# Reordering the first loads, the key transposes and one weight load in a fused adaLN attention and SwiGLU block

## The chip, the cores and the metric

The kernel runs on one core of one Trainium2 chip. The metric is device time in microseconds (us) of one execution, lower is better. Each run lists its mean granted TensorE clock.

The engines are called PE (TensorE), DVE (VectorE), ACT (ScalarE), POOL (GpSimd) and SP (the queue that issues most of the DMAs).

## The reference

All tensors are bfloat16. There are 2048 tokens of width 1024, 32 query heads and 4 key/value heads of width 128, a window of 512 keys, and a feed-forward width of 3584. Cut to what matters:

```python
mod = (silu(c) @ w_mod).reshape(1, 6, 1, -1)          # sa, ca, ga, sb, cb, gb
h = layernorm(x) * (1 + ca) + sa
q = h @ wq                                            # 32 heads of 128
k, v = k_cache[..., -512:, :], v_cache[..., -512:, :] # 4 heads, each used by 8 query heads
x = x + ga * (softmax(q @ k.T * 128**-0.5) @ v @ wo)
h = layernorm(x) * (1 + cb) + sb
x = x + gb * ((silu(h @ w_gate) * (h @ w_up)) @ w_down)
```

## The kernel before

The tokens are worked in four chunks of 512. The query weights `wq` come in groups of four heads (1 MB each). Keys must be transposed ("turned") once on PE, four 128x128 blocks for each of the 4 key groups, by way of one PSUM bank, `XB`. An iteration `i` of the attention loop computes scores of head `i-1` and the weighted values of head `i-2`, and projects a later head.

For the first chunk the projections of heads 0 to 7 start before the shift `sa` is known; their bias `wq.T @ sa` is added later, from the "bias columns" (matmuls of one column each). The parts that matter, with cuts:

```python
def wq_slot(gidx):                       # which of three SBUF slots a query group goes to
    return NWQ if gidx == 2 else gidx % NWQ          # NWQ = 2
...
for hf in range(2):                      # the loads at the start, all from SP, in order
    load_wca(hf); load_wq0(hf)
load_wq(1)
load_k(0)
for k2 in range(DT // 2):
    load_wsa(k2)
load_v(0)
load_wq(2)                               # 1 MB, third query group (heads 8 to 11)
load_x(1)                                # 1 MB, second tokens
for gk in range(1, Hkv):
    load_k(gk)                           # 128 KB each
for gk in range(1, Hkv):
    load_v(gk)
...
qproj_mm(7, QB0[7], 0, HK)               # just before the loop
q_bias_mm(0, 2, BB); q_shifted(0)        # bias columns of heads 0, 1, copied by DVE
qproj_mm(7, QB0[7], HK, DT); q_raw(7); q_shifted(1)
for dt in range(DT):
    shift(dt)                            # eight DVE operations, add sa to the input
...
for i in range(1, NA + 2):
    if i % 4 == 1 and i > 5 or i == 6:
        load_wq((i + 3) // 4 + 1)        # i == 6 loads the fourth query group (heads 12 to 15)
    ...
    for gk in {2: (1,), 3: (2, 3)}.get(i, ()):
        k_turn(gk, XB)                   # PE, into bank XB
        T.op(DVE, lambda: V.tensor_copy(kd, ks), writes=[PB[XB], B_kT[gk]])
    ...
    if i == 1: scores(0)
    if i in (1, 3, 5):
        q_bias_mm(i + 1, i + 3, QB)      # bias columns of the next two heads, in bank QB
    if i > NQ0: qproj(i + LEAD)          # NQ0 = 8, LEAD = 3
    elif i % 2 == 0: qproj(NQ0 - 1 + i // 2)   # i == 2 projects head 8, into bank QB
    ...
    scores(i - 1); pv(i - 2); run_bg(1)
```

The softmax here doesn't subtract the row's maximum and nothing guards it: scores larger than these inputs give would overflow.

## Time and profile before

| what | value |
|---|---|
| time, median of the first 3 runs | 1278.99 us (1278.6 to 1279.32) |
| span of the profiled execution | 1277.5 us |
| PE busy | 1259.3 us, 99% of the span |
| mean granted PE clock in that execution | 1.000 |

The first part of the page gives the busy time of each engine, its share of the span and its instructions.

```profile
PE 1259.3 (99%) x7541; PEld 646.0 (51%) x7683; DVE 480.1 (38%) x897; ACT 341.8 (27%) x388; POOL 42.2 (3%) x102
```

PE is the bound, so only the time that PE stands idle can be won by reordering. The list of waits of PE says for what it stood idle: total us, times, longest.

```profile
PE ps L272 <- DMA arena<-in_A_k_cache_dram: 2.2, 1, 2.2
PE ps L268 <- POOL arena L407: 2.2, 1, 2.2
PE ps L268 <- DMA arena<-in_A_wq_dram: 1.6, 2, 0.9
PE ps L272 <- DVE arena L853: 1.6, 1, 1.6
```

Line 268 is the helper of all matmuls, line 272 that of the PE transposes. The timeline of PE shows where these waits are (start, length, engine, line, operation, count, and in brackets the idle time before it and its releaser).

```profile
30.29 0.54 PE L268 MATMUL ps<-mod_bf,arena 128*128 128x1 bf16 x16
33.07 0.40 PE L272 MATMUL ps<-arena 128*128 128x128 bf16 x4 [2.24 <-DMA arena<-in_A_k_cache_dram]
33.30 3.66 PE L268 MATMUL ps<-arena 128*128 128x512 bf16 x27
36.80 0.39 PE L272 MATMUL ps<-arena 128*128 128x128 bf16 x4
38.78 0.38 PE L272 MATMUL ps<-arena 128*128 128x128 bf16 x4 [1.59 <-DVE arena L853]
...
44.67 0.54 PE L268 MATMUL ps<-mod_bf,arena 128*128 128x1 bf16 x16
...
57.52 1.90 PE L268 MATMUL ps<-arena 128*128 128x512 bf16 x7 [0.71 <-DMA arena<-in_A_wq_dram]
59.25 0.34 PE L268 MATMUL ps<-sc_bf,arena 128*128 128x1 bf16 x8
```

There are three stalls after 30 us (the POOL wait and the 0.9 us wait for a query load lie before 14 us, and the change does not touch them). At 30.8 us the turn of key group 1 (iteration 2) waits for its load. At 37.2 us the second of two turns in one bank (iteration 3) waits for DVE to copy out the first. At 56.8 us the projection of head 12 waits for the fourth query group. The timeline of DVE shows why the second took long: the copy of the turned keys (L853) stands in a queue.

```profile
37.00 0.18 DVE L774 RECIPROCAL rl<-ps 128x4 f32<-128x4 f32 x1 [1.08 <-PE ps L268]
37.22 0.69 DVE L777 TENSOR_TENSOR arena<-ps,rl 128x512 bf16<-128x512 f32 x1
37.83 0.47 DVE L665 TENSOR_SCALAR arena<-arena,bq 128x512 bf16<-128x512 f32 x1
38.22 0.41 DVE L853 COPY arena<-ps 128x512 bf16<-128x512 bf16 x1
```

The timeline of the SP queue shows when the two loads were issued.

```profile
22.99 3.03 SPq L384 DMA_DIRECT2D arena<-in_A_k_cache_dram  x3
...
49.51 0.52 SPq L354 DMA_DIRECT2D arena<-in_A_wq_dram  x1
```

Key group 1 landed 10.0 us after issue and the fourth query group 8.0 us after.

### The profile page before, as it was taken

How to read it: one execution, taken by the hardware profiler on the slowest of the kernel's cores; microseconds unless marked ns; L12 is line 12 of the kernel's file. 1: busy time of each engine (PE TensorE's matmuls, PEld its weight loads, DVE VectorE, ACT ScalarE, POOL GpSimd, SP SyncE). 2: the span in 40 equal slices, each digit the busy share in tenths (PEclk: the TensorE clock that was granted, in tenths of full speed). 3: DMA queues.
4: the chain of work that ended last, by engine and by line, in shares of the span. 5: the costliest groups of instructions: out<-in, count | busy, mean ns of one | idle time of the engine just before them, and what ended most of it. 6: DMA issues, size and time to landing. Idle time of an engine off the chain costs nothing.

```text
span 1277.5 us, 17800 instructions
## 1 busy us (share of the span) xinstructions
PE 1259.3 (99%) x7541; PEld 646.0 (51%) x7683; DVE 480.1 (38%) x897; ACT 341.8 (27%) x388; POOL 42.2 (3%) x102
## 2 busy tenths in 40 slices
PE   8899999999999999999999999999999999999999
PEld 5565545555455564465554444444444444444444
DVE  4555325765247652265422322233222331222222
ACT  4555303555025550055510111011100111011100
POOL 1011000000000010000000000000000000000000
PEclk9999999999999999999999999999999999999999
DMA  9899403977018741054252974046421654035200
GB/s 323 225 234 247 104 1 79 194 142 165 1 22 183 155 104 42 4 129 113 71 148 83 277 233 131 25 145 160 136 71 47 196 145 132 17 116 165 66 9 25
DMA packets 235854, 155.31 MB, mean 122 GB/s; under 512 B 129024, under 2 KB 222080, under 8 KB 235776
## 3 DMA queue, kind: packets, MB, share of 16 engines
q1 hardware_dynamic: 177520, 95.45, 31.4%
q10 hardware_dynamic: 58256, 58.73, 14.6%
q8 instruction: 60, 0.98, 0.3%
q14 instruction: 18, 0.15, 0.0%
HBM read 119.54 MB, written 4.19 MB: 97 GB/s over the span
## 4 chain that ended last, share of the span: by engine, by line
PE 96%; SPq 2%; DMA 1%; issue 1%; DVE 0%; ACT 0%
PE ps L268 96%; DMA arena<-in_A_k_cache_dram 1%; DMA arena<-in_A_wq_dram 1%; SPq L331 0%; SPq L299 0%; SPq L354 0%; SPq L384 0%; SPq L363 0%; SPq L306 0%; SPq L358 0%; ACT arena L756 0%; DVE rl L774 0%; PE ps L272 0%; SPq L389 0%; DVE arena L777 0%
## 5 line engine op out<-in xcount | busy, mean ns | idle before, releaser
L268 PE MATMUL ps<-arena 128*128 128x512 bf16 (+2 forms) x7236 | 1251.8, 333 | 11.5 <-POOL arena L407 2.2
L268 PEld LDWEIGHTS ps<-arena 128*128 128x128 bf16 x7378 | 635.8, 98 | 620.5 <-issue 2.5
L756 ACT ACTIVATE arena<-ps 128x1024 bf16<-128x1024 f32 x256 | 262.2, 1024 | 353.8 <-PE ps L268 342.1
L988 ACT ACTIVATE arena<-ps 128x512 bf16<-128x512 f32 x112 | 66.9, 597 | 506.4 <-PE ps L268 506.4
L989 DVE TENSOR_TENSOR arena<-ps,arena 128x512 bf16<-128x512 f32 x112 | 77.5, 692 | 276.6 <-PE ps L268 276.6
L796 DVE TENSOR_TENSOR tmp<-ps,rowb 128x512 f32<-128x512 f32 (+1 forms) x65 | 44.4, 683 | 318.7 <-PE ps L268 318.7
L639 DVE CAST arena<-ps 128x512 bf16<-128x512 f32 x120 | 83.0, 692 | 54.8 <-PE ps L268 54.8
L777 DVE TENSOR_TENSOR arena<-ps,rl 128x512 bf16<-128x512 f32 x128 | 88.5, 691 | 4.7 <-DVE rl L774 0.3
L774 DVE RECIPROCAL rl<-ps 128x4 f32<-128x4 f32 x128 | 23.4, 183 | 119.0 <-PE ps L268 119.0
L414 DVE BATCH_NORM_STATS2 st<-x_res 128x6 f32<-128x512 bf16 x62 | 42.3, 683 | 3.5 <-DMA x_res<-in_A_x_dram 3.4
L419 POOL TENSOR_SCALAR rstd<-mv 128x1 f32<-128x1 f32 x28 | 6.3, 227 | 891.7 <-DVE mv L418 891.7
L584 DVE SCALAR_TENSOR_TENSOR arena<-arena 128x1024 bf16<-128x1024 bf16 x24 | 29.2, 1215 | 0.0
L798 DVE TENSOR_TENSOR arena<-tmp,x_res 128x512 bf16<-128x512 f32 (+1 forms) x33 | 22.3, 676 | 1.1
L798 DVE TENSOR_TENSOR x_res<-tmp,x_res 128x512 bf16<-128x512 f32 x32 | 22.1, 692 | 1.1
L430 DVE TENSOR_SCALAR arena<-arena,gain,mod_bf 128x512 bf16<-128x512 bf16 x56 | 20.3, 405 | 0.0
L425 DVE TENSOR_SCALAR nsc<-x_res,mv,rstd 128x1024 bf16<-128x1024 bf16 x30 | 16.0, 534 | 0.0
L421 POOL TENSOR_TENSOR rstd<-rstd,mhalf 128x1 f32<-128x1 f32 x28 | 15.8, 565 | 2.3
L599 POOL TENSOR_SCALAR arena<-arena,c 128x128 bf16<-128x128 bf16 x24 | 14.4, 618 | 32.7 <-PE ps L268 32.4
L268 PEld LDWEIGHTS ps<-sc_bf,arena 128*128 128x128 bf16 x192 | 6.7, 96 | 2.3
L268 PE MATMUL ps<-sc_bf,arena 128*128 128x1 bf16 x192 | 6.8, 163 | 0.1
L272 PE MATMUL ps<-arena 128*128 128x128 bf16 x32 | 3.1, 218 | 3.8 <-DMA arena<-in_A_k_cache_dram 2.2
L418 DVE BATCH_NORM_AGGREGATE mv<-st 128x2 f32<-128x12 f32 x28 | 5.8, 209 | 1.0
(53 smaller groups left out, 50.4 us busy)
## 6 DMA issues: line engine op xcount, KB each, us to landing
arena<-in_A_wq_dram SPq DMA_DIRECT2D x31, 1024.0 KB, 6.1
arena<-in_B_w_gate_dram ACTq DMA_DIRECT2D x28, 1024.0 KB, 5.4
arena<-in_B_w_up_dram ACTq DMA_DIRECT2D x28, 1024.0 KB, 8.2
arena<-in_A_wo_dram SPq DMA_DIRECT2D x8, 1024.0 KB, 7.1
arena<-in_B_w_down_dram SPq DMA_DIRECT2D x7, 1024.0 KB, 8.7
out_dram<-arena SPq DMA_DIRECT2D x15, 256.0 KB, 2.0
x_res<-in_A_x_dram SPq DMA_DIRECT2D x3, 1024.0 KB, 7.7
arena<-in_w_mod_dram SPq DMA_DIRECT2D x8, 256.0 KB, 6.3
```

The lines of the kernel that those rows point to most:

```text
L268: T.op(PE, lambda: TE.matmul(out_ap, lhsT, rhs, start=start, stop=stop, skip_group_check=skip), reads=reads, writes=[bank_buf])
L414: T.op(DVE, lambda: V.bn_stats(st_[sl][:, hf * 6:hf * 6 + 6], x_res[:, t, hf * 512:hf * 512 + 512]), reads=[B_x[t]], writes=[B_st[sl]])
L430: T.op(DVE, lambda: V.tensor_scalar(dst[:, dt, :], dst[:, dt, :], gain[gi][:, dt:dt + 1], mod_bf[:, ccol + dt:ccol + dt + 1], op0=ALU.mult ...
L584: T.op(DVE, lambda: V.scalar_tensor_tensor(mt[n % 2], mt[n % 2], 1.0, sc_row, op0=ALU.mult, op1=ALU.mult, accum_out=mcol[:, n:n + 1]), rea ...
L639: T.op(DVE, lambda: V.tensor_copy(qT_s[qs], bank(b)), writes=[PB[b], B_qT[qs]])
L756: T.op(ACT, lambda: A.activation(ex_s[es][:, 2 * kp:2 * kp + 2, :], banks2(SCB + 2 * kp), AF.Exp, scale=att_scale), writes=[PB[SCB + 2 * k ...
L774: T.op(DVE, lambda: V.reciprocal(rl[r][:, :].rearrange("p (a b) -> p a b", a=2), psap(PVB * 512 + P, [[512, 2], [130, 2]])), writes=both + ...
L777: T.op(DVE, lambda: V.tensor_tensor(o_s[os_].rearrange("p (a b) d -> p a b d", a=2), psap(PVB * 512, [[512, 2], [130, 2], [1, P]]), rlb, A ...
L796: T.op(DVE, lambda: V.tensor_tensor(tmp[s][:, 0:n], bank(b, n), rowb[ri][:, c0:c0 + n], ALU.mult), reads=[B_row[ri]], writes=[PB[b], B_tmp ...
L798: T.op(DVE, lambda: V.tensor_tensor(dst[:, c0:c0 + n], tmp[s][:, 0:n], x_res[:, t, c0:c0 + n], ALU.add), reads=[B_tmp[s], B_x[t]], writes= ...
L988: T.op(ACT, lambda: A.activation(sg_s[ss], bank(gb), AF.Silu), writes=[PB[gb], B_sg[ss]])
L989: T.op(DVE, lambda: V.tensor_tensor(guT[:, ft, :], bank(ub), sg_s[ss], ALU.mult), reads=[B_sg[ss]], writes=[PB[ub], B_gu[ft]])
```

## The change

Its intent is to take away the three stalls. Key group 1 is read before the third query group, and the second tokens last. One key group is turned per iteration, so that DVE has an iteration to empty the bank. The fourth query group goes into the first slot, whose last reader (the bias columns of heads 2 and 3) is in iteration 1, so it can be issued at iteration 4 instead of 6. Later groups alternate between the first two slots, as before but with the parity turned round.

```diff
             def wq_slot(gidx):
-                return NWQ if gidx == 2 else gidx % NWQ
+                return gidx if gidx <= NWQ else (gidx + 1) % NWQ
@@
             load_v(0)
+            load_k(1)
             load_wq(2)
-            load_x(1)
-            for gk in range(1, Hkv):
+            for gk in range(2, Hkv):
                 load_k(gk)
             for gk in range(1, Hkv):
                 load_v(gk)
+            load_x(1)
@@
-                if i % 4 == 1 and i > 5 or i == 6:
-                    load_wq((i + 3) // 4 + 1)
+                if i % 4 == 1 and i > 5 or i == 4:
+                    load_wq((i + 4) // 4 + 1)
@@
-                for gk in {2: (1,), 3: (2, 3)}.get(i, ()):
+                for gk in {2: (1,), 3: (2,), 4: (3,)}.get(i, ()):
```

## The prediction

> **What bounds it now.** TensorE: the busy table gives 1259.3 us of a 1277.5 us span (99%), granted clock full, and PE is 96% of the chain of waits. Only idle PE time near the start can be won: the table by stretches shows 3.96 us idle between 30 and 40 us, 0.84 us between 50 and 60 us. The list of waits and the PE timeline name three stalls:
> 1. 30.83 to 33.07 us: the turns (PE transposes) of key group 1, iteration 2, wait for its DMA (2.24 us). Issued at 22.99 us behind wq group 2 and the second tokens (1 MB each), it took 10.0 us.
> 2. 37.2 to 38.8 us, iteration 3: groups 2 and 3 are turned in one bank; the second turn waits for the copy of the first, queued on DVE behind reciprocal 0.18, normalisation 0.69, shift 0.47, own copy 0.41 us. Idle 1.59 us.
> 3. 56.8 to 57.5 us: wq group 3, issued at 49.51 us, landed 8.0 us later; PE idle 0.71 us.
>
> **What changes.** Nothing is added or removed, only order. Key group 1 is issued before wq group 2; other keys and values before the second tokens; one turn moves from iteration 3 to 4; wq group 3 goes to slot 0, read last at iteration 1, and is issued at iteration 4.
>
> **DMA check.** [...] a 128 KB key load took 10.0 us behind megabytes. Key 1, now issued near 16.7 us, should land by 27 us, before 30.83. wq group 2 (landed 28.85) is pushed by 128 KB at 368 GB/s, 0.35 us: 29.2 us, before use near 31.9. Second tokens should land by about 34 us, read near 45. wq group 3: issued about 41, landed by 50, wanted about 53.
>
> **What each step is worth.**
> 1. Not all of 2.24 us. After the turn (0.23) comes head 8's projection into the bank of the bias matmuls, whose copy by DVE ends at 31.93 us behind eight shifts. So it starts at about 31.98 instead of 33.30 us: 1.3 us saved, and a new stall of about 0.7 us on DVE.
> 2. From turn to turn is 1.98 us; a free turn takes 0.22: 1.75 us saved. Exponentials (2.14 us a head on ACT) come close to limiting here; I allow 0.2 us lost.
> 3. 0.7 us saved.
> Sum about 3.6 us, all on the critical path, since PE has no large gaps afterwards and everything merely starts earlier.
>
> **Predicted time** 1275.4 us, 8 in 10 between 1273.8 and 1277.6 us. Faster by over 2%: 0.01; within 2%: 0.98; slower by over 2%: 0.01.
>
> **Signs.** Right: no PE wait on a key DMA; at iteration 2 a PE wait of 0.5 to 0.9 us on DVE (bias copy or shifts) after the turn; none on key copies at 35 to 40 us; none on wq at 50 to 60 us; PE idle from 30 to 60 us down from about 5 to about 1.3 us; PE busy still near 1259 us. Wrong: PE waits on wq group 2 at 31 to 33 us, on ACT at 36 to 40 us, or DVE statistics waiting for second tokens near 45 us.
>
> **What would make it wrong.** wq group 2 later than its margin of 2.7 us; stall 2 returning as a wait on score banks held by ACT (0.5 us at 45.7 us now); the gate columns (1 MB) and wq group 3 colliding near 40 us and delaying head transposes and the modulation matmuls of iteration 7. Any of these would shrink the gain to 2 us or less; none costs a per cent.

One clause of the DMA check is cut from the record. No term of the sum (1.3, 1.75 less 0.2, and 0.7 us, about 3.6 us) rested on it, and the landing of key group 1 near 27 us is an estimate from its issue near 16.7 us and the 10.0 us of the first trace.

## The result, and the profile after

The changed kernel took 1275.52 us (median of 4 runs, 1275.35 to 1275.87); the kernel before took 1279.15 us (median of 4, 1278.6 to 1280.52). The ratio is 0.997, 95% interval 0.9953 to 0.9988: within 2%, and faster. Ratios here are the mean time of one kernel's runs over that of the other's in the same rounds, so they are not quite the ratio of the medians quoted.

The span fell from 1277.5 to 1273.8 us. The busy line of the page after:

```profile
PE 1267.0 (99%) x7683; PEld 645.7 (51%) x7683; DVE 479.6 (38%) x897; ACT 341.5 (27%) x388; POOL 42.0 (3%) x102
```

PE busy time rose by 7.7 us although no matmul was added. The count behind it explains that: the trace before has 7541 PE records and the trace after 7683, as many as there are weight loads in both. 142 matmul records are missing from the first trace, and PE busy time may not be compared between these two.

The waits of PE after:

```profile
PE ps L268 <- POOL arena L408: 2.2, 1, 2.2
PE ps L268 <- DVE bq L661: 1.0, 1, 1.0
PE ps L268 <- DMA arena<-in_A_wq_dram: 0.7, 1, 0.7
```

The wait on the key load and the wait on the copy between turns are gone. The 0.7 us on a query load that is left is an older one between 9 and 14 us, which was 0.9 us in the trace before. A new wait of 1.0 us on DVE has come up. The timeline of PE after, at the same places:

```profile
30.39 0.54 PE L268 MATMUL ps<-mod_bf,arena 128*128 128x1 bf16 x16
30.80 0.38 PE L272 MATMUL ps<-arena 128*128 128x128 bf16 x4
32.17 3.66 PE L268 MATMUL ps<-arena 128*128 128x512 bf16 x28 [0.99 <-DVE bq L661]
35.66 0.39 PE L272 MATMUL ps<-arena 128*128 128x128 bf16 x4
...
38.07 0.39 PE L272 MATMUL ps<-arena 128*128 128x128 bf16 x4
...
41.79 0.54 PE L268 MATMUL ps<-mod_bf,arena 128*128 128x1 bf16 x16
...
55.49 0.34 PE L268 MATMUL ps<-sc_bf,arena 128*128 128x1 bf16 x8
```

And the issue of key group 1, on SP, which now lands 10.1 us later, at 26.8 us:

```profile
16.69 2.88 SPq L384 DMA_DIRECT2D arena<-in_A_k_cache_dram  x1
```

To keep the three steps apart I use four marks that all these kernels share in the timeline of PE: A, the bias columns of iteration 1 (30.29 us before); B, the projection of head 8 (33.30); C, the bias columns of iteration 5 (44.67); D, the first eight gate columns of iteration 9 (59.25). Step 1 lies between A and B, step 2 between B and C, step 3 between C and D.

| | A to B | B to C | C to D |
|---|---|---|---|
| before | 3.01 | 11.37 | 14.58 |
| after | 1.78 | 9.62 | 13.70 |
| gain | 1.23 | 1.75 | 0.88 |

The sum is 3.86 us; mark A was 0.10 us later in this execution, which leaves 3.76 us at mark D. The span is 3.7 us shorter. So everything after 60 us merely starts earlier: the two traces agree there, and the gain is neither lost nor increased later.

### The profile page after: what moved, and what is told of

Its sections match the earlier page's. It is cut to its first block, busy times and chain, and to the rows that moved or that the text cites. A ratio compares the mean times of both kernels' runs of the same rounds, so it can differ in the third digit from the quotient of the medians.

```text
span 1273.8 us, 17943 instructions
## 1 busy us (share of the span) xinstructions
PE 1267.0 (99%) x7683; PEld 645.7 (51%) x7683; DVE 479.6 (38%) x897; ACT 341.5 (27%) x388; POOL 42.0 (3%) x102
## 4 chain that ended last, share of the span: by engine, by line
PE 99%; DMA 1%; DVE 0%; SPq 0%; ACT 0%; issue 0%
PE ps L268 98%; DMA arena<-in_A_wq_dram 1%; DVE arena L671 0%; SPq L331 0%; SPq L306 0%; PE ps L272 0%; ACT arena L757 0%; DVE arena L666 0%; DVE tmp L797 0%; DVE arena L799 0%; DVE bq L661 0%
## 5 line engine op out<-in xcount | busy, mean ns | idle before, releaser
L268 PE MATMUL ps<-arena 128*128 128x512 bf16 (+1 forms) x7378 | 1260.7, 334 | 4.0 <-POOL arena L408 2.2
L640 DVE CAST arena<-ps 128x512 bf16<-128x512 f32 x120 | 82.9, 691 | 53.8 <-PE ps L268 53.8
L653 DVE COPY arena<-ps 128x512 f32<-128x512 f32 x4 | 2.7, 688 | 8.3 <-PE ps L268 8.3
```

The lines of the kernel that those rows point to most:

```text
L268: T.op(PE, lambda: TE.matmul(out_ap, lhsT, rhs, start=start, stop=stop, skip_group_check=skip), reads=reads, writes=[bank_buf])
L640: T.op(DVE, lambda: V.tensor_copy(qT_s[qs], bank(b)), writes=[PB[b], B_qT[qs]])
```

## The experiments

The theory is that there are three separate stalls, each removed by one part of the change. The rivals are that the parts only pay together, that ACT or the DMA takes the gain back, or that something later in the kernel is the cause. A fourth question came up: why the times of the kernel before spread much more than those of the changed one.

### Each part alone

The load order alone (the second hunk of the diff, on the kernel before):

> Only the order of the first loads is that of the changed kernel (key group 1 before the third wq group, second tokens last). Theory of three separate stalls: the wait on the key DMA at 30.8 us is gone and a PE wait of about 1.0 us on the DVE bias copy stands in its place, so the projection of head 8 starts at 32.2 instead of 33.3 us, 1.1 us gained; the wait of 1.6 us for the copy of the second turn and the 0.7 us on the fourth wq group stay. Time 1.1 us below before. Rival (the parts only pay together, because PE catches up with the next late thing): a start earlier by 1.1 us is eaten by a longer wait at the double turn or on the fourth wq group (which lands at a fixed time), time within 0.4 us of before.

The turns alone (the last hunk):

> Only the turns are moved: one key group per iteration at 2, 3 and 4. Three separate stalls: the 2.24 us wait on the key DMA stays, the 1.6 us wait for the copy between two turns is gone, the bias matmuls of iteration 3 start 1.75 us earlier counting from the first turn; 1.75 us below before. Rival (exponentials on ACT limit these iterations): PE waits on ACT for score banks grow by about as much and the gain is under 0.7 us.

The fourth query group alone (the first and third hunks):

> Only the fourth wq group goes to the first slot and is loaded at iteration 4. Three separate stalls: the wait of 0.7 us at 57 us (0.9 on the weight load) is gone, nothing before it moves, 0.8 us below before. Rival (the load is DMA bound, its bytes collide with the gate columns and landings move out): the wait stays over 0.4 us, or a new wait on gate columns appears at 50 us, time within 0.3 us of before.

All three gave correct results. The kernel before, in the rounds of these runs, had a median of 1280.47 us (7 runs, 1278.57 to 1282.52).

| run | times, us | median | A to B | B to C | C to D |
|---|---|---|---|---|---|
| load order alone | 1277.9 to 1280.06 | 1278.32 | 1.78 | 11.36 | 14.95 |
| turns alone | 1276.89 to 1277.38 | 1277.11 | 1.96 | 9.63 | 15.03 |
| fourth group alone | 1277.33 to 1277.77 | 1277.69 | 2.37 | 11.36 | 13.70 |

Each part takes its own stretch to the value that the changed kernel has there (1.78, 9.62 and 13.70 us) and, but for two things told below, leaves the others alone. That the parts pay only together is refuted, and so is a gain taken back by ACT: the turns alone gave the full 1.74 us. The marks are used here, and not the times, because 5 of the 7 runs of the kernel before in these rounds had a lower clock (0.999 to 0.997, see below); against its two runs at full clock (1278.9 and 1278.57 us) the three medians are 0.4, 1.6 and 1.0 us lower.

Two numbers were not as expected. First, two of these kernels have the load order of before, yet they waited less for the key load than its first trace: A to B took 1.96 and 2.37 us instead of 3.01. Second, C to D grew where the fourth query group was not touched, from 14.58 to 14.95 and 15.03 us: when PE arrives earlier, part of the gain goes into a longer wait for that group. The rival of a longer wait for that group later on has a grain of truth, of about 0.4 us.

### How much of it is chance

The kernel before, unchanged, profiled again:

> The kernel before, unchanged, profiled once more. The first experiments that kept its load order waited 1.18 and 1.59 us for key group 1 where its own first trace shows 2.24 us. If the landing of that load varies from run to run, this trace shows a wait between 1.0 and 2.4 us at 30.8 us that is not 2.24, the other two stalls as before (1.6 us at the turn exactly, 0.6 to 1.2 us on the fourth wq group), and the times spread over more than 1 us. Rival (2.24 us is what the order costs, and the two parts each removed some of it): 2.2 us again and a spread under 0.7 us.

Its median was 1279.85 us (1278.64 to 1280.65, 4 runs); A to B took 2.35 us, with a wait of 1.57 us for the keys:

```profile
32.02 0.40 PE L272 MATMUL ps<-arena 128*128 128x128 bf16 x4 [1.57 <-DMA arena<-in_A_k_cache_dram]
```

B to C took 11.36 and C to D 14.90 us. So the wait for the key load varies from execution to execution with the landing of a load that sits behind megabytes: 2.24 us in the first trace, 1.57 here, 1.18 in the turns alone, 1.59 in the fourth group alone; it landed 10.0, 8.9, 9.3 and 8.9 us after its issue. The turn's stall is the same every time (B to C is 11.36 or 11.37 us in the four traces that have it). The first trace happened to show a large step 1 and a small step 3.

### Undoing one part

The changed kernel with the first loads in the old order:

> The changed kernel with the loads at the start in the old order (key group 1 after the second tokens). Separate stalls: a wait on the key DMA of 1.2 to 2.2 us at 30.8 us comes back in place of the 1.0 us on the bias copy, nothing else; 0.2 to 1.2 us slower than the changed kernel, and times that spread more. Rival (the order feeds later loads too): also a wait on the fourth wq group or on gate columns, over 1.5 us slower.

The changed kernel with the new slot but the old time of issue of the fourth query group:

```diff
-                if i % 4 == 1 and i > 5 or i == 4:
-                    load_wq((i + 4) // 4 + 1)
+                if i % 4 == 1 and i > 5 or i == 6:
+                    load_wq((i + 3) // 4 + 1)
```

> The changed kernel, with the fourth wq group still in the first slot but issued at iteration 6 as before. If what counts is when it is issued, the wait of PE on it comes back at 53 us, at 1.0 to 1.3 us (more than the 0.7 us of before, as PE arrives earlier after the two other stalls are gone), and the kernel is about 1.2 us slower than the changed one. Rival (what counts is the slot, whose old readers held the load back): wait under 0.3 us, time equal to the changed kernel.

The changed kernel with the second tokens back in their old place:

```diff
             load_k(1)
             load_wq(2)
+            load_x(1)
             for gk in range(2, Hkv):
@@
-            load_x(1)
```

> The changed kernel, with the second tokens loaded after the third wq group as before, so that only key group 1 goes ahead. With one turn per iteration, key group 2 is wanted at 35.7 us and should land at 33 to 34.5 us, so nothing waits and the time equals the changed kernel within 0.3 us: second tokens last is then worth nothing. Rival: a wait on the key DMA of up to 1 us at 35.7 us.

All were correct. The kernel before had a median of 1279.09 us in these rounds (7 runs).

| run | times, us | median | A to B | B to C | C to D |
|---|---|---|---|---|---|
| old load order | 1275.96 to 1277.57 | 1276.64 | 2.56 | 11.31 | 13.70 |
| fourth group issued late | 1276.27 to 1276.99 | 1276.79 | 1.78 | 9.62 | 15.21 |
| second tokens kept | 1275.06 to 1275.86 | 1275.31 | 1.78 | 9.62 | 13.70 |

The late issue brings this wait back, in the list of waits of PE of that run:

```profile
PE ps L268 <- DMA arena<-in_A_wq_dram: 1.3, 1, 1.3
```

It is what counts about the third part: with the new slot and the old time of issue C to D takes 15.21 us, so the early issue is worth 1.5 us by the traces, twice what the wait of 0.71 us before promised, and 1.1 us by the mean times (1276.71 against 1275.57, in different jobs). A wait in the list also tells a little less than it costs: in all five traces told of so far that have this wait, C to D exceeds 13.70 us by the listed wait plus 0.17 us (0.71 gives 0.88, 1.34 gives 1.51). The free first slot is only what allows that issue. Putting the second tokens last is worth nothing that these runs can see: with them in their old place the time is 1275.31 us against 1275.52.

With the old load order the wait for the key load came back in place of the one on DVE, and the mean time was 1.1 us longer than the changed kernel's (1276.70 against 1275.57), both as expected:

```profile
32.19 0.40 PE L272 MATMUL ps<-arena 128*128 128x128 bf16 x4 [1.79 <-DMA arena<-in_A_k_cache_dram]
```

But it gave a surprise. Its B to C took 11.31 us, 1.7 us more than the 9.62 us of the same turns, with no wait for an engine or a load to account for it. The stretches of that trace show it (stretch, length, then busy us and instruction counts of PE, weight loads, DVE, ACT and POOL, then the granted PE clock, the DMA share and GB/s):

```profile
25.00:30.00 5.00, 4.87 (x70) 2.79 (x70) 2.48 (x8) 0.97 (x2) 0.00 (x0) 1.00 1.07 368
30.00:35.00 5.00, 2.99 (x27) 1.50 (x25) 2.41 (x9) 1.68 (x2) 0.00 (x0) 0.75 0.98 281
35.00:40.00 5.00, 5.00 (x63) 3.39 (x62) 2.36 (x6) 3.09 (x4) 0.00 (x0) 0.91 0.14 52
```

The clock that PE was granted fell to 0.75 of full in the mean of the five microseconds that hold the end of the wait. In finer stretches it was 1.00 during the wait, 0.50 from 32.5 to 35.9 us, and then 1.00 again. The weight loads, one for each matmul, show the spacing:

```profile
32.19 0.23 PEld L272 LDWEIGHTS ps<-arena 128*128 128x128 bf16 x4 [1.87 <-DMA arena<-in_A_k_cache_dram]
...
33.20 0.15 PEld L268 LDWEIGHTS ps<-arena 128*128 128x128 bf16 x1 [0.28 <-issue]
33.63 0.15 PEld L268 LDWEIGHTS ps<-arena 128*128 128x128 bf16 x1 [0.28 <-issue]
...
35.76 1.83 PEld L268 LDWEIGHTS ps<-arena 128*128 128x128 bf16 x19 [0.28 <-issue]
```

They are 0.43 us apart until about 35.8 us, where matmuls of this size otherwise are about 0.22 us apart (the eight of head 12's projection take 1.90 us, the last drawn 0.38 us long). So at a granted clock of 0.50 the spacing doubled, for 3.4 us. The drop followed a wait of 1.79 us here, while in the first trace of the kernel before a wait of 2.24 us was not followed by one (granted clock 1.00 in every stretch from 28 to 41 us). Whether the wait brought it about, this trace alone does not tell.

### Is the spread of the kernel before the clock?

Since each run lists its mean granted clock, all 29 later runs of the kernel before can be sorted by it (25 beside other kernels, 4 of its second profiling).

| mean granted clock | runs | times, us | mean, us |
|---|---|---|---|
| 1.000 | 15 | 1278.33 to 1279.8 | 1278.88 |
| 0.999 to 0.997 | 14 | 1280.06 to 1283.48 | 1280.88 |

The two heaps do not overlap: about half of the executions have a lower clock, and they take 2.0 us longer. Twelve of them, at 0.999 and 0.998, average 1280.53 us, 1.65 us above the others, which is about what the one slow stretch in the trace above cost (1.7 us); the two at 0.997 took 1282.52 and 1283.48 us. None of these slower executions was profiled, so whether one of the three stalls lets the clock drop, and which, is not shown. All 4 runs of the changed kernel have 1.000, but so have the 8 runs of "turns alone" and "fourth group alone", which keep the wait for the key, while one of the 4 runs of "load order alone", which does not have it, was at 0.998 (1280.06 us). Four runs each are too few to tell. Whether a wait can bring the drop about is tested by filling the wait with work.

The kernel before, with matmuls on zeros ahead of the turn at iteration 2 (a second line keeps the zeros safe from a later load into their place):

```diff
+                if i == 2:
+                    warm(6, XB)
                 for gk in {2: (1,), 3: (2, 3)}.get(i, ()):
@@
-                    for b_ in B_qT[NQT:]:
+                    for b_ in B_qT[NQT:] + [B_zw]:
```

> The kernel before, with 6 matmuls on zeros (about 1.3 us) put in front of the turn of key group 1 at iteration 2, where PE otherwise idles for its DMA. The times of the kernel before fall in two heaps, near 1278.7 and near 1280.6 us, and the profile of the changed kernel with late keys shows PE at half rate (matmuls 0.43 us apart, granted clock 0.75 of full between 30 and 35 us) after that wait. Theory (the idle of 1.2 to 2.2 us lets the clock drop in about half of the executions, at 1.7 to 2 us each): the wait for the key ends as late as before, but the upper heap is gone: all runs within 1278.2 to 1279.5 us, median about 0.5 to 1 us below before. Rival (the upper heap is loads that land later): both heaps stay, spread over 1.5 us, median as before or higher.

The same kernel made worse on purpose, and then filled with 14 such matmuls:

```diff
-            for gk in range(1, Hkv):
+            for gk in range(2, Hkv):
                 load_k(gk)
             for gk in range(1, Hkv):
                 load_v(gk)
+            load_k(1)
```

> The kernel before, with key group 1 loaded after all values, on purpose worse: the wait at the turn grows from 1.2 to 2.2 to about 3.5 to 5 us. Theory of the clock: the clock drops in every execution, granted clock under 0.8 in the stretch after the wait, matmuls 0.43 us apart for 2 to 4 us; time about 1283 us: about 3 us of added wait over the lower heap of before (1278.7), and 1.7 to 2 us for the clock. Rival (the clock does not follow the wait): granted clock 1.0, time about 1281.5 us in one heap.

> As the run with key group 1 loaded after all values, with 14 matmuls on zeros (3.0 us) in front of its turn. Theory of the clock: the wait ends at the same time, no matmuls 0.43 us apart, granted clock 1.0 throughout, 1.5 to 2.5 us faster than without the filling, although it does more work. Rival: same time as without the filling.

All three were correct; the kernel before had a median of 1279.61 us (11 runs, 1278.52 to 1283.48).

| run | times, us | mean, us | clock of each run |
|---|---|---|---|
| before, filled | 1278.65 to 1280.14 | 1279.43 | 1.000 in all 6 |
| key group 1 last | 1282.71 to 1285.58 | 1284.64 | 0.997, 0.996, 0.998, 0.996 |
| key group 1 last, filled | 1281.92 to 1283.59 | 1282.91 | 1.000, 0.999, 1.000, 0.999 |

The stretches of the profiled execution of "key group 1 last", first, and of the same one filled:

```profile
35.00:40.00 5.00, 4.95 (x30) 2.66 (x29) 0.94 (x3) 1.87 (x2) 0.00 (x0) 0.66 0.22 84
40.00:45.00 5.00, 3.23 (x36) 2.25 (x35) 2.14 (x6) 1.74 (x3) 0.00 (x0) 0.75 0.35 84
```

```profile
35.00:40.00 5.00, 3.71 (x32) 2.18 (x30) 2.56 (x6) 2.05 (x2) 0.00 (x0) 1.00 0.27 107
40.00:45.00 5.00, 4.62 (x50) 3.02 (x52) 2.39 (x7) 2.05 (x2) 0.00 (x0) 1.00 0.67 200
```

The turn of iteration 2 in these two traces:

```profile
34.34 0.40 PE L272 MATMUL ps<-arena 128*128 128x128 bf16 x4 [3.30 <-DMA arena<-in_A_k_cache_dram]
```

```profile
34.59 0.40 PE L272 MATMUL ps<-arena 128*128 128x128 bf16 x4 [0.53 <-DMA arena<-in_A_k_cache_dram]
```

Unfilled, with a wait of 3.30 us in the profiled run (3.5 to 5 had been expected), the clock dropped in every run (0.996 to 0.998 in the mean), and the mean of 1284.64 us is above the 1283 expected. In the profiled run the granted clock was 0.66 in the mean from 35 to 40 us, and 0.75 from 40 to 45 us, after the second stall. The weight loads of that trace are 0.43 us apart from about 35.7 to 38.7 us, and again from 42.7 to 44.0 us. If the clock was 0.50 while it was low, as in the trace with the old load order, it was low for 3.4 us before 40 us and for 2.5 us before 45 us (an estimate from the two means). Neither slow stretch begins at once when PE is back at work, at 34.34 and 41.73 us: about 1.3 and 0.8 us later by these figures. What sets when it begins, and why the wait of 2.24 us in the first trace was not followed by a drop, is not shown.

With the wait filled, PE did 14 matmuls more and the kernel was 1.7 us faster in the mean (the times of the two overlap by 0.9 us, their clocks do not); two of its four runs had 0.999, where 1.000 throughout had been expected, and their second stall was not filled. The two turns of iterations 2 and 3 started at 34.34 and 39.75 us unfilled and at 34.59 and 38.32 us filled. That idle PE time brings the clock drop is thus shown for this long wait: from 35 to 40 us the granted clock was 0.66 unfilled and 1.00 filled. In the kernel before, filled, none of 6 runs had a lower clock, where 4 of the 11 unfilled runs beside them had (14 of 29 in all).

The second half of that expectation failed: the filled runs reach 1280.14 us, and no gain in time is shown (mean 1279.43 against 1279.83 of the 11 runs beside them; ratio 0.9996, 95% interval 0.9984 to 1.0008). The 7 of those 11 that kept full clock average 1279.09 us, so the filled runs are 0.34 us above them; why is open. The filled runs still wait for a key that lands at a varying time (0.35 us beyond the filling in the profiled one, where it landed 9.0 us after its issue). Filling a stall is therefore poor medicine here: the clock stayed at 1.000 in 6 of 6 runs, but the wait is kept. Removing the stall takes away the wait, and all 4 runs of the changed kernel had a clock of 1.000.

### The wait that was left

The new stall of 0.99 us in the changed kernel, predicted as about 0.7 us, is a bank: head 8's projection goes into bank `QB`, which holds the bias columns of heads 2 and 3 until DVE has copied them, and DVE runs the eight shifts first (2.18 us from 29.77 us on; the copy ends at 32.03 us, and the projection starts at 32.17 us). The edit does those columns together with the first two, before the shifts, in another bank:

```diff
-            q_bias_mm(0, 2, BB)
+            q_bias_mm(0, 4, BB)
@@
-                    if i in (1, 3, 5):
+                    if i in (3, 5):
```

> The changed kernel, with the bias matmuls of heads 2 and 3 done together with those of heads 0 and 1, before the eight shifts, so that the bank of head 8's projection is free long before. If the new stall of 1.0 us at iteration 2 is the bank held by the bias copy behind the shifts, the projection of head 8 starts right after the turn, the wait is under 0.2 us and the time falls by about 0.8 to 1.0 us below the changed kernel, 4.5 us below before. Rival (the projection waits for the shifts of its own input, or for the third wq group, landed at 29.8 us): the start stays within 0.2 us of 32.17 us and nothing is gained; or the first scores are delayed by the two extra bias columns and the gain is given back there.

It was correct and took 1274.34 us (median of 4, 1274.04 to 1275.07), 0.9954 of the kernel before (0.9939 to 0.9969) and about 1.1 us below the changed kernel (mean of 4 runs 1274.45 against 1275.57, in different jobs). Its timeline of PE:

```profile
30.00 1.04 PE L268 MATMUL ps<-arena 128*128 128x512 bf16 x4 [0.21 <-DVE arena L666]
30.88 0.39 PE L272 MATMUL ps<-arena 128*128 128x128 bf16 x4
31.10 3.66 PE L268 MATMUL ps<-arena 128*128 128x512 bf16 x28
```

The projection follows the turn at once, at 31.10 instead of 32.17 us. It reads the shifted input block by block, and the shifts, which end later (eight in 2.18 us from 30.26 us on), stay ahead of it: no wait is listed there.

One more step was tried, the bias columns after the third block of head 7's projection instead of the fourth, to take away the 0.21 us in front of the first scores:

```diff
-            qproj_mm(7, QB0[7], 0, HK)
+            qproj_mm(7, QB0[7], 0, 3)
@@
-            qproj_mm(7, QB0[7], HK, DT)
+            qproj_mm(7, QB0[7], 3, DT)
```

> The changed kernel with the four bias columns done together early, and these put after the third instead of the fourth step of head 7's projection, as the first scores waited 0.2 us for the shifted query of head 0. Expected: that wait falls from 0.21 us to under 0.1 us, time 1.0 to 1.3 us below the changed kernel, so 1274.2 us, at most 0.2 us below the version with the split at four. Rival: the bias matmuls wait for the modulation column instead and nothing is gained over the version with the split at four.

It took 1274.81 us (1274.27 to 1276.08), no gain in time. From the start of the bias columns to the turn it is 2.91 us in both traces, though the wait of 0.21 us is no longer listed. One of its 4 runs had a clock of 0.999 and was the slowest; where in that run PE idled no profile shows. The version with the split at four has the lowest median, though the two overlap.

## Why the prediction was right or wrong

The time was right: 1275.4 us predicted, 1275.52 measured.

- **Three stalls, all on the critical path, later work merely starts earlier.** Right. The single parts changed their own stretch (and C to D grew by about 0.4 us where PE came earlier to the old issue of the fourth group), and the 3.76 us won by mark D became 3.7 us of span.
- **Step 1, 1.3 us, with a new stall behind the bias copy.** Right in mechanism: 1.23 us in the traces, and the new wait was 0.99 us on the copy that the prediction named, slightly above its 0.5 to 0.9. The key load took 10.0 us to land behind megabytes and again 10.1 us when issued 6.3 us earlier, so it moved by as much as its issue. But the 2.24 us wait it was read from was the largest of the five of this load order: over these, A to B averages 2.45 us, so the typical gain is 0.7 us.
- **Step 2, 1.75 us less 0.2 for ACT.** 1.75 us: B to C is 9.62 or 9.63 us in every trace that has the new turns and no slow clock there. ACT took nothing.
- **Step 3, 0.7 us.** Too small: 0.88 us in the traces, and 1.5 us when only this part is undone. The prediction read it as a fixed wait, but with the two other stalls gone PE arrives 3.0 us earlier (53.8 instead of 56.8 us, in the run with the late issue) at a load whose landing comes forward by 2.4 us only.
- **Missing: the clock.** The prediction treated the clock as full, as its one trace showed. In about half of the executions of the kernel before it was lower, and these took 2.0 us longer. Against runs at full clock the change wins 3.3 us (1278.88 to 1275.57), against the mean of all 29 runs 4.3 us (1279.85). That the predicted 3.6 us came out is in part luck: step 1 was read 0.6 us too large, step 3 at 0.7 us was too small (0.88 to 1.5 us), the 0.2 us set aside for ACT were not lost, and these errors nearly cancel. The missing clock did little harm to the predicted time, because its starting point, 1278.99 us, is a median of three runs (1278.6 to 1279.32 us) that all lie in the range of the full-clock heap.
- **Signs.** The waits named as gone are gone, and none of the PE waits named as wrong came. PE busy near 1259 us failed, as the first trace lacked 142 records. PE idle from 30 to 60 us went from 4.95 to 1.05 us, against 1.3 predicted, with the same caution.

## What to carry to other kernels

A small load that is wanted early belongs ahead of the megabytes that are wanted later, because its landing moved with its issue: here the 128 KB of key group 1 landed 8.9 to 10.5 us after issue in either place, in twelve traces, so an issue 6 us earlier made a landing about 6 us earlier. Two uses of one PSUM bank in one iteration cost the wait for all that stood in the DVE queue between them, 1.75 us here; spread over two iterations they cost nothing (no such wait is listed after). When a profile shows one idle gap on PE, look at the granted clock of several runs before putting a price on it: in this kernel a gap of 2 us could cost about 4 us (an estimate: the gap plus the 1.7 us of one slow stretch), and then only in some executions.
